# Attention and a gated MLP in one kernel: the softmax maxima reach the query rows by sixteen direct transfers, from an earlier place, in a new order of a period's products

## The chip, the cores and the metric

The kernel runs on one core of one Trainium2 chip. The metric is device time in microseconds for one execution; before the change it is 1812.37 us (median of 3 runs, 1811.87 to 1816.35). Five engines matter: PE (TensorE, matrix products, with its weight loads PEld), DVE (VectorE), ACT (ScalarE), POOL (GpSimd) and SP (SyncE), which here only issues DMA transfers from one queue.

## The reference

```python
x = A_x                                             # [1, 2048, 512], float32
g = sigmoid((x * gate_w).sum(-1, keepdims=True))
# a: full attention, 32 heads of 16
qkv = (x @ wqkv).reshape(B, S, 3, 32, 16).transpose(2, 0, 3, 1, 4)
p = softmax(einsum("bhqd,bhkd->bhqk", q, k) * 16 ** -0.5)
a = einsum("bhqk,bhkd->bhqd", p, v).transpose(0, 2, 1, 3).reshape(B, S, 512) @ wo
# b: gated MLP, 512 -> 1792 -> 512
b = (sigmoid(x @ w_gate) * (x @ w_up)) @ w_down
return g * a + (1 - g) * b
```

Both branches read the same `x`. Every score row needs its own maximum before the exponential.

## The kernel before, in words

**Pairs, halves, periods.** Two heads form a pair `p` (16 pairs): one uses the lower 64 rows of the PE array (`b = 0`), the other the upper 64 (`b = 1`). A pair's 2048 queries are two halves `i` of 1024. The main loop runs over 256 periods `k`; eight periods handle one half of one pair. The queries of a pair lie in a tile `QS` with heads along partitions, the keys in `KS`.

**Maxima by an extra row.** The scores are computed twice. Ten periods ahead (`FIRST = 20` steps), `sm_step` forms them with queries along partitions (L250) and DVE takes row maxima (L252) into `stat`; after 64 of them a last reduction (L256) yields `m`, the maxima of one half: 128 partitions, 2 heads, 8 blocks of 128 queries. Later `st_part` forms the scores again, transposed, with keys along partitions (L460), and ACT exponentiates them out of PSUM (L462). So that nothing has to be subtracted there, each head's query rows in `QS` carry two more rows (partitions `64 b + 48` and `64 b + 49`) with the maximum, split in a high and a low part, and the key rows carry -1 against them. These two rows per head must be in `QS` before the first transposed product of a half.

**The way of the maxima.** `split_max` (L260) splits `m` into `mhl` on POOL (a cast, L94, and a subtraction, L95). `turn_max` (L265) transposes `mhl` in 32 x 32 blocks on DVE (L269), stores the result to a DRAM buffer `m_d` (L270, 16 KB) and loads it back into the four rows of `QS` (L275, four loads of 4 KB each, in pieces of 128 bytes), `b = 0` first. All transfers are issued by SP, in one order.

**A period.** `emit` (L517) walks through the words of `STEADY`, one product each: `t0` and `t1` are transposed scores of the two heads (`t1` one period ahead of `t0`), `m0` and `m1` score products for maxima, `d0` and `d1` halves of a dense product (`Sum`) in the bank `dn` that belongs to the projections and to the MLP. The suffix is the half of the PE array; products of different halves run at once. A dense product has 12 terms and takes two periods. `turn` stands for a POOL no-op that hands `dn` from one half to the other, for one piece of queued POOL work, and for `turn_max` if a split is waiting. After the words come the next dense run, two more pieces of POOL work (`work(2)`), and `values(k)` (L467): eight products of probabilities with `v`, on all 128 rows. At the very end `split_max` is recorded.

**Banks.** Apart from `dn`, seven PSUM banks serve the 17 products of a period that need one. `place` (L511) hands them out: `REUSE` says for each of the 17 places how many hand-outs back its bank was last given. A product waits until the bank's former reader (ACT for `t` and values, DVE for `m`) is done.

**Order.** PE, ACT, DVE and POOL run in the order in which the code is written; SP's order is set by the scheduler. In the first 48 periods the dense products are projections of q and k: their results are split by POOL (L120, L117) and stored by SP (L207). Later ones are MLP columns, stored at L305. `load_pair` (L210) loads the next pair's rows.

In the prediction, the turn period is the one after a half's maxima are complete, in which the transpose is done; the stall period is the next, in whose middle the first `t1` needs the new rows.

Of the kernel before, what the change touches and what calls it, by code (L numbers as in the profile page):

```python
# [11 lines left out]
F32 = mybir.dt.float32  # L12
F32R = mybir.dt.float32r
# [11 lines left out]
P = 128  # L25
# [4 lines left out]
NPAIR = H // 2  # L30
# [13 lines left out]
def gated_mix(ctx, tc, x, xc, wqk, wv, wo, w_gu, w_down, gate_w, out):  # L44
    nc = tc.nc
    pe, act, dve, pool, sp = nc.tensor, nc.scalar, nc.vector, nc.gpsimd, nc.sync

    ctx.enter_context(tc.manual_schedule(engines=ORDERED))
    keep = ctx.enter_context(tc.tile_pool(name="keep", bufs=1))
    dram = ctx.enter_context(tc.tile_pool(name="dram", bufs=1, space=DRAM))  # L50
# [18 lines left out]
    gu_d = dram.tile([2, NF, P, S], F32, name="gu_d")  # L69
    pv_d = dram.tile([2, NPAIR, P, 512], F32, name="pv_d")  # L70
    rec_d = dram.tile([P, 512], F32, name="rec_d")
    m_d = dram.tile([NPAIR, 2, P, 32], F32, name="m_d")

    warm = keep.tile([P, 1], F32, name="warm")
    dve.memset(warm, 0.0)
# [14 lines left out]
    def split(h, l, src, hi, lo):  # L90
        if hi is act:
            act.activation(h, src, AF.Copy)  # L92
        else:
            hi.tensor_copy(h, src)  # L94
        lo.tensor_tensor(l, src, h.bitcast(F32), ALU.subtract)  # L95
# [72 lines left out]
    QS, KS = zip(*[(big(f"qs{b}", F32R), big(f"ks{b}", F32R)) for b in range(2)])  # L168
# [64 lines left out]
    mrow = {}  # L233
# [24 lines left out]
        return one  # L258

    def split_max(half):  # L260
        hl = keep.tile([P, 2, 16], F32R, name=f"mhl{half[0]}_{half[1]}", tag="mhl", bufs=2)
        split(hl[:, 0, :], hl[:, 1, :], mrow.pop(half).rearrange("p a b -> p (a b)"), pool, pool)
        turning.append((half, hl))

    def turn_max():  # L265
        half, hl = turning.pop(0)
        p, i = half
        mt = keep.tile([P, 32], F32, name=f"mt{p}_{i}", tag="mt", bufs=2)
        dve.transpose(mt, hl.rearrange("p a b -> p (a b)").bitcast(F32))  # L269
        sp.dma_start(m_d[p, i], mt)  # L270
        rows = m_d[p, i].rearrange("(g a b t) j -> a b t g j", g=4, a=2, b=2)
        for b in range(2):
            for a in range(2):
                r = 64 * b + 3 * DH + a
                sp.dma_start(QS[p % 2][r:r + 1, i * 1024:(i + 1) * 1024].bitcast(F32).rearrange(  # L275
                    "o (t g j) -> o t g j", g=4, j=32), rows[a, b].unsqueeze(0))

    turning = []

# [45 lines left out]
    for c in range(NC):  # L325
# [9 lines left out]
        for w, dst in ((w_q, q_d), (w_k, k_d)):  # L335
            o = bank()
# [20 lines left out]
    for t in range(2):  # L357
        o = bankv()
# [90 lines left out]
    def st_part(k, b):  # L449

        p, r = divmod(2 * k, 32)
        i, kt = divmod(r, 16)
        qs, ks = QS[p % 2], KS[p % 2]
        r = 64 * b
        pt = ptile[k, b] = mid(f"p{k}_{b}")
        for a in range(2):
            for c in range(2):
                o = bank()
                q0 = i * 1024 + c * 512
                pe.matmul(o, ks[r:r + KR, (kt + a) * P:(kt + a + 1) * P], qs[r:r + KR, q0:q0 + 512],  # L460
                          start=True, stop=True)
                act.activation(pt[:, 2 * a + c, :], o, AF.Exp, scale=DH ** -0.5)  # L462
                yield
# [47 lines left out]
    def place():  # L511
        b = given[-REUSE[count_given[0] % len(REUSE)]]
        count_given[0] += 1
        given.append(b)
        return b

    def emit(order, **parts):  # L517

        for word in order.split():
            if word == "turn":  # L520
                turn(run)
                work(1)
                if turning:
                    turn_max()
            else:
                next(parts[word], None)

    STEADY = ("t0 m1 d1 m0 t0 d1 d1 m0 d1 t0 d1 m0 d1 turn t0 t1 m0 "
              "d0 m1 m1 d0 d0 t1 d0 t1 t1 d0 d0 m1")
    REUSE = (5, 8, 6, 6, 10, 7, 7, 6, 8, 7, 7, 6, 8, 6, 8, 7, 7)  # L530
    LAST = ["t0 d1 t0 d1 t0 d1 d1 turn t0 t1 t1 d0 t1 d0 t1 d0 d0"] * (TAIL - 4) + [
        "t0 d1 t0 d1 t0 d1 turn t0 t1 t1 d0 t1 d0 t1 d0"] * 4

# [10 lines left out]
    for k in range(NPER):  # L544
        n = 2 * k
        if n + FIRST == NSTEP:
            bank = bank7
            leave = dve.tensor_copy
        if 128 <= n < 256 and n % 16 == 0:
            logit_load((n - 128) // 8)  # L550
        if 128 <= n < 256 and n % 16 in (6, 8):
            logits((n - 128) // 16 * 2, (n % 16 - 6) // 2)
        if n % 32 == 0 and n // 32 + 1 < NPAIR:
            load_pair(n // 32 + 1)
        parts["t0"], parts["t1"] = st_part(k, 0), st_part(k + 1, 1) if k + 1 < NPER else iter(())
        emit(STEADY if k < NPER - TAIL else LAST[k - NPER], **parts)
        if k == NPER - 1:
            bankd = bank
        if run.done():
            run = next(fill)  # L560
        else:
            turn(run)
        work(2)
        if k == NPER - 1:
            break
        values(k)
        for half in list(mrow):
            split_max(half)
        if n == NSTEP - 16:
            loaded.extend(hidden_load(*chunks[m]) for m in range(2))  # L570
            raws = [late_raw(*late[m][:2]) for m in range(2)]
        if n == NSTEP - 10:
            denominators(0)
# [86 lines left out]
    for n, (c, f) in enumerate(chunks):  # L660
# [4 lines left out]
        hl = ready[n]  # L665
# [49 lines left out]
```

## Time and profile before

| | |
|---|---|
| median of 3 runs | 1812.37 us (1811.87 to 1816.35) |
| the profiled execution | 1814.77 us, span 1813.0 us |
| mean granted TensorE clock | 0.991 |
| PE busy | 1753.0 us, 97% of the span |
| DVE, ACT, POOL busy | 1417.8, 1341.6, 467.6 us |
| from 260 to 1000 us of the span | PE 713.91, DVE 631.28, ACT 610.63 of 740 us |
| waits of PE for the maxima rows | 34.3 us (20 times) and 18.0 us (11 times) |

The span runs from the first to the last instruction; the execution's own time lies 1.8 us above it. Rows of a timeline give start, duration, engine, line, operation and, in brackets, how long the engine stood idle before and what ended it; `x4` merges four instructions. Rows of stretches give the stretch, its length, busy time and count of PE, PEld, DVE, ACT and POOL, then the granted TensorE clock, the share of the DMA engines and GB/s. A DMA row on SPq is the time of issue, not of the transfer.

### The profile page before, as it was taken

The numbers are of one execution on the slowest core, as the hardware profiler recorded it, in microseconds if no ns is written. First come the engines' busy times: TensorE is split into PE (matmuls) and PEld (weight loads), VectorE is DVE, ScalarE is ACT, GpSimd is POOL, SyncE is SP. The second block draws the span as 40 slices with busy tenths as digits, with TensorE's granted clock in tenths as the row PEclk, the third lists the DMA queues.
The fourth block names the chain that finished last, engine by engine and source line by source line (L and its number), as shares of the span: only waits on it lengthen the run. The fifth ranks groups of instructions, "written<-read, shape, count | busy, mean of one in ns | idle before, by whom it ended". The sixth has DMA issues, their size and how long they took to land.

```text
span 1813.0 us, 33225 instructions
## 1 busy us (share of the span) xinstructions
PE 1753.0 (97%) x12676; PEld 1046.7 (58%) x12676; DVE 1417.8 (78%) x2282; ACT 1341.6 (74%) x2564; POOL 467.6 (26%) x435
## 2 busy tenths in 40 slices
PE   9999999999999999999999999999999999999999
PEld 7755555555555555555555555555555555488887
DVE  5987787788888888888888888888888887156543
ACT  4187787788888888788888888888888888953321
POOL 1034343332222222222222222222222222352110
PEclk9999999999999999999999999999999999999999
DMA  9212324141313131313131212112121212277752
GB/s 253 68 37 65 77 65 89 48 112 37 72 48 83 48 83 48 78 48 82 38 65 43 59 49 56 46 51 55 45 54 45 63 43 77 72 237 245 249 187 74
DMA packets 84959, 149.22 MB, mean 82 GB/s; under 512 B 18816, under 2 KB 27008, under 8 KB 81792
## 3 DMA queue, kind: packets, MB, share of 16 engines
q1 hardware_dynamic: 84512, 146.58, 29.6%
q8 instruction: 99, 1.62, 0.4%
q14 instruction: 60, 0.49, 0.1%
q10 hardware_dynamic: 288, 0.52, 0.1%
HBM read 87.56 MB, written 59.51 MB: 81 GB/s over the span
## 4 chain that ended last, share of the span: by engine, by line
PE 84%; DMA 6%; DVE 5%; SPq 3%; issue 1%; ACT 0%; POOL 0%; POOLq 0%
PE dn L143 14%; PE sm L475 13%; PE sm L460 11%; PE st L475 10%; PE sm L250 8%; PE st L460 8%; PE sm L670 7%; DVE stat L252 5%; PE st L250 4%; PE st L130 4%; SPq L275 3%; DMA qs<-m_d 3%; DMA m_d<-mt 3%; PE dn L670 2%; PE st L143 1%; PE sm L579 1%
## 5 line engine op out<-in xcount | busy, mean ns | idle before, releaser
L252 DVE TENSOR_REDUCE stat<-sm 128x1 f32<-128x512 f32 x1188 | 766.3, 681 | 110.0 <-PE sm L250 85.5
L462 ACT ACTIVATE p<-sm 128x512 f32<-128x512 f32 x1190 | 675.4, 622 | 35.9 <-PE st L250 26.5
L252 DVE TENSOR_REDUCE stat<-st 128x1 f32<-128x512 f32 x860 | 567.4, 680 | 119.7 <-PE st L250 101.4
L490 POOL TENSOR_TENSOR sum<-sum,part 128x512 f32<-128x512 f32 x224 | 287.9, 1285 | 920.5 <-PE sm L460 624.7
L462 ACT ACTIVATE p<-st 128x512 f32<-128x512 f32 x858 | 498.4, 623 | 24.6 <-PE st L250 13.8
L460 PE MATMUL sm<-qs,ks 64*128 64x512 f32 x1190 | 476.2, 424 | 35.1 <-DMA qs<-m_d 34.3
L250 PE MATMUL sm<-ks,qs 48*128 48x512 f32 x1188 | 475.1, 435 | 0.2
L250 PE MATMUL st<-ks,qs 48*128 48x512 f32 x860 | 364.4, 445 | 0.0
L460 PE MATMUL st<-qs,ks 64*128 64x512 f32 x858 | 342.7, 419 | 19.9 <-DMA qs<-m_d 18.0
L460 PEld LDWEIGHTS sm<-qs,ks 64*128 64x128 f32 x1190 | 221.0, 186 | 215.8 <-ACT p L462 97.0
L475 PE MATMUL sm<-p,v 128*17 128x512 f32 x2096 | 250.7, 595 | 0.0
L250 PEld LDWEIGHTS sm<-ks,qs 48*128 48x128 f32 x1188 | 214.1, 186 | 51.3 <-DVE stat L252 31.8
L475 PE MATMUL st<-p,v 128*17 128x512 f32 x2000 | 242.4, 602 | 0.0
L460 PEld LDWEIGHTS st<-qs,ks 64*128 64x128 f32 x858 | 159.0, 186 | 120.6 <-ACT p L462 49.8
L250 PEld LDWEIGHTS st<-ks,qs 48*128 48x128 f32 x860 | 155.2, 186 | 29.7 <-DVE stat L252 20.5
L479 ACT ACTIVATE part<-st 128x512 f32<-128x512 f32 x124 | 75.2, 607 | 103.8 <-issue 88.6
L475 PEld LDWEIGHTS sm<-p,v 128*17 128x17 f32 x2096 | 48.8, 97 | 122.9 <-issue 81.5
L475 PEld LDWEIGHTS st<-p,v 128*17 128x17 f32 x2000 | 46.6, 97 | 122.0 <-issue 84.4
L479 ACT ACTIVATE part<-sm 128x512 f32<-128x512 f32 x100 | 61.7, 617 | 67.4 <-issue 63.1
L424 DVE TENSOR_TENSOR gul<-gul 128x1024 f32<-128x1024 f32 (+1 forms) x30 | 46.0, 1538 | 35.0 <-ACT gul L423 32.4
L670 PE MATMUL sm<-wd_h,hl 128*128 128x512 f32 x208 | 68.3, 395 | 0.0
L92 ACT ACTIVATE hl<-gul 128x1024 fp32r<-128x1024 f32 (+1 forms) x30 | 29.9, 996 | 43.4 <-PE sm L670 29.7
(455 smaller groups left out, 2998.7 us busy)
## 6 DMA issues: line engine op xcount, KB each, us to landing
gu_d<-gu SPq DMA_DIRECT2D x112, 256.0 KB
gul<-gu_d SPq DMA_DIRECT2D x56, 512.0 KB
qs<-q_d SPq DMA_DIRECT2D x90, 128.0 KB
ks<-k_d SPq DMA_DIRECT2D x90, 128.0 KB
pv_d<-sum SPq DMA_DIRECT2D x32, 256.0 KB
q_d<-qe SPq DMA_DIRECT2D x12, 512.0 KB
k_d<-qe SPq DMA_DIRECT2D x12, 512.0 KB
x<-in_xc_dram SPq DMA_DIRECT2D x16, 256.0 KB
```

Of the source, the lines that this page charges most:

```text
L130: pe.matmul(o, a, b, start=(i == 0), stop=(i == len(ops) - 1))
L143: mm = pe.matmul(self.o, a[rows], b[rows], start=(self.n == 0), stop=(self.n == 2 * len(self.ops) - 1))
L250: pe.matmul(t, qs[r:r + KM, qt * P:(qt + 1) * P], ks[r:r + KM, g * 512:(g + 1) * 512], start=True, stop=True)
L252: dve.tensor_reduce(stat[half][:, b, qt % 8, g:g + 1], t, axis=AX.X, op=ALU.max)
L275: sp.dma_start(QS[p % 2][r:r + 1, i * 1024:(i + 1) * 1024].bitcast(F32).rearrange("o (t g j) -> o t g j", g=4, j=32), rows[a, b].unsqueeze(0))
L424: dve.tensor_tensor(gu[:, 1, a], gu[:, 0, a], gu[:, 1, a], ALU.mult)
L460: pe.matmul(o, ks[r:r + KR, (kt + a) * P:(kt + a + 1) * P], qs[r:r + KR, q0:q0 + 512], start=True, stop=True)
L462: act.activation(pt[:, 2 * a + c, :], o, AF.Exp, scale=DH ** -0.5)
L475: pe.matmul(o[32 * c:32 * c + VW, :], v[:, 2 * k % 16 + a, h * VW:(h + 1) * VW], pts[c // 2][:, 2 * a + c % 2, :], start=(a == 0), stop=(a ...
L479: act.activation(e, o, AF.Copy)
L490: pool.tensor_tensor(s, s, e, ALU.add)
L670: pe.matmul(down[t], a, b, start=(f == 0 and m == 0), stop=(f == NF - 2 and m == 5))
```

## The change

Four things change. `split_max` is recorded before a period's end work instead of after `values(k)`. `turn_max` is recorded at the start of the next period, before its first product, instead of at `turn` in its middle. The buffer `m_d` goes: `mhl` is laid out so that 8 partitions of the transposed tile hold the pieces of one row for one residue `g`, and sixteen transfers go straight from the transposed tile to the rows of `QS`, each 8 pieces of 128 bytes. And `STEADY` and `REUSE` get new values.

```diff
-    m_d = dram.tile([NPAIR, 2, P, 32], F32, name="m_d")
...
     def split_max(half):
-        hl = keep.tile([P, 2, 16], F32R, name=f"mhl{half[0]}_{half[1]}", tag="mhl", bufs=2)
-        split(hl[:, 0, :], hl[:, 1, :], mrow.pop(half).rearrange("p a b -> p (a b)"), pool, pool)
+        hl = keep.tile([P, 2, 2, 8], F32R, name=f"mhl{half[0]}_{half[1]}", tag="mhl", bufs=2)
+        split(hl[:, :, 0, :], hl[:, :, 1, :], mrow.pop(half), pool, pool)
         turning.append((half, hl))
 
     def turn_max():
         half, hl = turning.pop(0)
         p, i = half
         mt = keep.tile([P, 32], F32, name=f"mt{p}_{i}", tag="mt", bufs=2)
-        dve.transpose(mt, hl.rearrange("p a b -> p (a b)").bitcast(F32))
-        sp.dma_start(m_d[p, i], mt)
-        rows = m_d[p, i].rearrange("(g a b t) j -> a b t g j", g=4, a=2, b=2)
+        dve.transpose(mt, hl.rearrange("p b a t -> p (b a t)").bitcast(F32))
         for b in range(2):
             for a in range(2):
                 r = 64 * b + 3 * DH + a
-                sp.dma_start(QS[p % 2][r:r + 1, i * 1024:(i + 1) * 1024].bitcast(F32).rearrange(
-                    "o (t g j) -> o t g j", g=4, j=32), rows[a, b].unsqueeze(0))
+                row = QS[p % 2][r:r + 1, i * 1024:(i + 1) * 1024].bitcast(F32).rearrange(
+                    "o (t g j) -> o t g j", g=4, j=32)
+                for g in range(4):
+                    c = 32 * g + 16 * b + 8 * a
+                    sp.dma_start(row[:, :, g, :], mt[c:c + 8, :])
...
             if word == "turn":
                 turn(run)
                 work(1)
-                if turning:
-                    turn_max()
             else:
                 next(parts[word], None)
 
-    STEADY = ("t0 m1 d1 m0 t0 d1 d1 m0 d1 t0 d1 m0 d1 turn t0 t1 m0 "
-              "d0 m1 m1 d0 d0 t1 d0 t1 t1 d0 d0 m1")
-    REUSE = (5, 8, 6, 6, 10, 7, 7, 6, 8, 7, 7, 6, 8, 6, 8, 7, 7)
+    STEADY = ("t0 m1 d1 m0 t0 d1 m0 d1 d1 t0 d1 m0 d1 turn t0 t1 m0 "
+              "m1 d0 d0 t1 m1 d0 d0 t1 d0 t1 d0 m1")
+    REUSE = (6, 5, 9, 6, 9, 7, 7, 6, 8, 6, 8, 6, 8, 6, 8, 7, 7)
...
         parts["t0"], parts["t1"] = st_part(k, 0), st_part(k + 1, 1) if k + 1 < NPER else iter(())
+        if turning:
+            turn_max()
         emit(STEADY if k < NPER - TAIL else LAST[k - NPER], **parts)
+        for half in list(mrow):
+            split_max(half)
         if k == NPER - 1:
             bankd = bank
         if run.done():
...
         values(k)
-        for half in list(mrow):
-            split_max(half)
```

What moves on the engines, at the places of which the prediction speaks. DVE at the turn of pair 7's second half, before the change (`stat` are the maxima of one half, `m` their last reduction, `mhl` the split, `mt` the transposed tile; the names `sm` and `st` on the right are PSUM banks):

```order
L256 TENSOR_REDUCE m_1_8472<-stat_1_7980 128x16
L252 TENSOR_REDUCE stat_0_8493<-st_67 128x1
L252 TENSOR_REDUCE stat_0_8493<-st_65 128x1
L252 TENSOR_REDUCE stat_0_8493<-st_66 128x1
L252 TENSOR_REDUCE stat_0_8493<-sm_69 128x1
L269 STREAM_TRANSPOSE mt_1_8514<-mhl_1_8487 128x32
L252 TENSOR_REDUCE stat_0_8493<-st_65 128x1
```

and with the change:

```order
L255 TENSOR_REDUCE m_1_8636<-stat_1_8151 128x16
L268 STREAM_TRANSPOSE mt_1_8654<-mhl_1_8638 128x32
L251 TENSOR_REDUCE stat_0_8675<-sm_72 128x1
L251 TENSOR_REDUCE stat_0_8675<-sm_69 128x1
L251 TENSOR_REDUCE stat_0_8675<-sm_71 128x1
```

The transpose moves from behind the fourth maximum of the next half to straight behind the reduction.

SP at the same place, before (`gu_d` is the store of an MLP column):

```order
L305 DMA gu_d<-gu_1_0_8474 128x512
L270 DMA m_d<-mt_1_8514 128x32
L275 DMA qs_108<-m_d 1x32x32 x4
L99 DMA g6r<-in_w_gu_dram 128x512
L305 DMA gu_d<-gu_1_1_8605 128x512
```

and with the change:

```order
L305 DMA gu_d<-gu_1_0_8641 128x512
L276 DMA qs_107<-mt_1_8654 1x8x32 x16
L98 DMA g6r<-in_w_gu_dram 128x512
L305 DMA gu_d<-gu_1_1_8780 128x512
```

One store and four loads become sixteen transfers at the same place of the queue.

SP in the first phase, second half of pair 1, with the change (`q_d` is the store of a projected and split q; before, it stood ahead of the store to `m_d`):

```order
L206 DMA k_d<-qe_0_2253 128x2x512
L276 DMA qs_107<-mt_1_2395 1x8x32
L206 DMA q_d<-qe_1_2381 128x2x512
L276 DMA qs_107<-mt_1_2395 1x8x32 x15
L206 DMA k_d<-qe_1_2523 128x2x512
```

Fifteen of the sixteen transfers stand behind the store of q, which waits for POOL. This is so in six halves: the second of pair 0, both of pairs 1 and 2, and the first of pair 3.

## The prediction

> **What bounds the kernel now.** I read the waits first, then stretches of single periods, then the timeline round one turn of maxima, then the issue times of the transfers. Busy time by engine from the page, and four rows of the waits (total us, times, longest):
>
> ```profile
> PE 1753.0 (97%) x12676; PEld 1046.7 (58%) x12676; DVE 1417.8 (78%) x2282; ACT 1341.6 (74%) x2564; POOL 467.6 (26%) x435
> ...
> PE sm L460 <- DMA qs<-m_d: 34.3, 20, 3.4
> PE st L460 <- DMA qs<-m_d: 18.0, 11, 2.8
> ...
> PEld sm L250 <- DVE stat L252: 31.8, 136, 0.4
> PEld st L250 <- DVE stat L252: 20.5, 92, 0.2
> ```
>
> TensorE sets the end. It loses 52.3 us in 31 waits for the maxima that come back into the query rows, one per half pair, and about 0.23 us in nearly every period (228 waits) for a PSUM bank that VectorE still reads. Four consecutive periods, stretch and length first, PEclk third from last; then the sum lines of the same view over the six stall periods of the first phase (two of them shown whole) and over the 24 after it:
>
> ```profile
> 879.62:885.23 5.61, 5.61 (x48) 3.15 (x44) 5.01 (x9) 5.05 (x10) 1.29 (x1) 1.00 0.01 3
> 885.23:890.87 5.64, 5.64 (x48) 3.14 (x44) 5.05 (x10) 4.58 (x9) 1.71 (x3) 1.00 0.14 49
> 890.87:897.75 6.88, 5.66 (x50) 3.16 (x46) 4.96 (x8) 5.22 (x10) 3.10 (x3) 1.00 0.09 11
> ...
> 131.75:143.45 11.70, 8.29 (x48) 4.11 (x45) 5.06 (x8) 5.22 (x10) 3.14 (x3) 0.71 0.01 1
> 182.75:192.38 9.63, 7.08 (x48) 4.08 (x44) 5.06 (x8) 5.22 (x10) 2.13 (x3) 0.82 0.27 44
> ...
> sum 58.03, PE 42.18 PEld 22.18 DVE 30.16 ACT 31.31 POOL 13.86; mean PE 7.03 PEld 3.70 DVE 5.03 ACT 5.22 POOL 2.31
> ...
> sum 171.98, PE 136.75 PEld 75.45 DVE 119.36 ACT 125.25 POOL 52.36; mean PE 5.70 PEld 3.14 DVE 4.97 ACT 5.22 POOL 2.18
> ```
>
> An ordinary period takes 5.61, the turn period (second row) 5.64, the stall period after it 6.88. Turn and stall period together cost 5.64 + 171.98/24 = 12.81 in 24 halves and 5.64 + 58.03/6 = 15.31 in the six early ones. The timeline of that turn, from T = 885.23 (the row of a DMA is from the chain of waits):
>
> ```profile
> 885.10 0.22 DVE L256 TENSOR_REDUCE m<-stat 128x16 f32<-128x64 f32 x1
> 885.23 0.50 PE L460 MATMUL st<-qs,ks 64*128 64x512 f32 x1
> 885.38 0.20 POOL L94 CAST mhl<-m 128x16 fp32r<-128x16 f32 x1 [2.33 <-DVE m L256]
> 885.66 0.22 POOL L95 TENSOR_TENSOR mhl<-m,mhl 128x16 fp32r<-128x16 f32 x1
> 885.80 1.29 DVE L252 TENSOR_REDUCE stat<-st 128x1 f32<-128x512 f32 x2 [0.48 <-PE st L250]
> 888.20 0.20 DVE L269 STREAM_TRANSPOSE mt<-mhl 128x32 f32<-128x32 f32 x1
> 888.33 0.65 DVE L252 TENSOR_REDUCE stat<-st 128x1 f32<-128x512 f32 x1
> 888.43 0.32 SPq L270 DMA_DIRECT2D m_d<-mt  x1
> 889.85 2.78 SPq L275 DMA_DIRECT2D qs<-m_d  x4
> 891.98 1.90 DMA qs<-m_d
> 892.39 0.40 PE L460 MATMUL sm<-qs,ks 64*128 64x512 f32 x1
> 894.01 0.47 PE L460 MATMUL sm<-qs,ks 64*128 64x512 f32 x1 [1.22 <-DMA qs<-m_d]
> ```
>
> The split is done at T+0.65, but the transpose stands in the middle of the period (T+2.97). The store lands, four loads are issued one each 0.695 (2.78 and a gap, over 4), the last lands at 893.88, 1.25 after its issue ends (891.98 + 0.65), and TensorE goes on 0.13 later, at T+8.78. Without a stall the matmul would come 0.23 after the one at 892.39: the stall is 1.39, and 3.74 remain to the period's end (897.75).
>
> **The change, part by part.** *Earlier turn.* VectorE now transposes straight after the last maxima, so it waits for POOL's T+0.65: from about T+0.70 to T+0.90. The next maxima queue behind it; their first read moves from T+0.57 to about T+0.83 (the transpose costs 0.13 net, 888.20 to 888.33). The products that end a period wait for the fifth read, so the turn period grows to about 5.80. The first matmul that needs the new rows stands 1.73 into a period (892.62 less 890.87), so without a stall it is due at T+5.80+1.73 = T+7.53. POOL's earlier place costs nothing in this phase: it stood idle 2.33 before the split.
>
> *Sixteen direct transfers.* The store (0.32 and 1.1 of landing) and four loads go; the first new issue can start at T+0.93. All is decided by what one issue costs, since the first stalled matmul needs the upper rows, which are the last eight of sixteen on SP's one queue. No row shows a transfer from SBUF to SBUF. Issue times of groups (min/median/max ns), and six issues in a row:
>
> ```profile
> L216 SPq DMA_DIRECT2D qs<-q_d x102: 302/418/797, 23.8 to 1410.1; - x102
> L275 SPq DMA_DIRECT2D qs<-m_d x128: 649/650/814, 79.7 to 1541.2; - x128
> L442 SPq DMA_DIRECT2D xn<-in_x_dram x8: 383/384/500, 397.6 to 733.0; - x8
> L621 SPq DMA_DIRECT2D ot<-pv_d x32: 577/577/641, 1608.6 to 1768.7; - x32
> ...
> 944.85 2.73 SPq L216 DMA_DIRECT2D ks<-k_d  x6
> ```
>
> Below: 302, the shortest issue of all, one each 0.347 with the gap of 45 ns that lies between issues. Above: 649, today's write of the same kind of row in the same 128-byte pieces. In a run, 16-row loads go out one each 0.463 (2.73 over 6, gap included), 418 apiece. L275 and L621 are the groups whose outermost size is 8 on one side; L621 costs about 200 more than L442, which has 128 there and as many dimensions. The new transfers are 8 pieces on both sides: shaped simply like L216, but with the 8. 302 + 200 gives 502, the run's price 418; I take 0.46, so one each 0.505.
>
> [...]
>
> *Sum of a turn.* The rows arrive at 0.93 + 15 x 0.505 + 0.46 + 1.20 + 0.13 = T+10.30 (1.20 for the landing: 1.25 above, 1.10 for the store, whose issue ends at 888.75 and which frees the loads at 889.85). Turn and stall period: 10.30 + 3.74 = 14.04 instead of 12.81: +1.23. The stall is 10.30 - 7.53 = 2.77, about 2.6 of idleness.
>
> *Clock.* In the early stall periods idleness is length less PE busy. At 2.55 and 3.41 (rows above) PEclk fell to 0.82 and 0.71, and PE's busy time rose from 5.6 to 7.08 and 8.29: +1.5 and +2.7. The third of the six shows the other side:
>
> ```profile
> 231.71:239.57 7.86, 5.56 (x49) 3.01 (x45) 4.96 (x8) 5.22 (x10) 1.53 (x2) 1.00 0.02 4
> 378.27:386.37 8.10, 5.58 (x50) 3.05 (x46) 4.96 (x8) 5.22 (x10) 1.54 (x2) 1.00 0.30 53
> ```
>
> 2.30 and 2.52 idle cost nothing. At 2.6 I count +1.5. [...]
>
> *Order of a period.* An ordinary period, from 914.51, on PE, VectorE, ScalarE and the weight loads:
>
> ```profile
> 914.51 0.50 PE L460 MATMUL sm<-qs,ks 64*128 64x512 f32 x1
> 916.43 0.50 PE L250 MATMUL st<-ks,qs 48*128 48x512 f32 x1
> ...
> 915.69 2.47 DVE L252 TENSOR_REDUCE stat<-st 128x1 f32<-128x512 f32 x4
> ...
> 915.19 2.56 ACT L462 ACTIVATE p<-sm 128x512 f32<-128x512 f32 x5
> ...
> 918.28 0.13 PEld L475 LDWEIGHTS st<-p,v 128*17 128x17 f32 x8 [0.30 <-DVE stat L252]
> ```
>
> The first maxima matmul after the period's middle (916.43) waits for VectorE's second read to end (915.69 + 0.68 = 916.37). In the new bank numbers it follows a bank that ScalarE's second exponential leaves at 915.19 + 0.49 + 0.60 = 916.28: 0.09 sooner. The closing products still take the bank of the fifth read, which ends at 918.16; with the same 0.06 they could start at 918.21 instead of 918.28. The gain is between 0 and 0.09 a period; I take 0.06, so 0.36 in the six ordinary periods of a half. If other banks come late instead, nothing hides it: 0.06 worse would cost 245 x 0.06 = 15 us.
>
> *The six early halves.* There the split of a projected q, two long POOL instructions, stood before the maxima; now it stands behind them, and its store stands on SP after the first of the sixteen:
>
> ```profile
> 176.81 0.61 POOL L120 CAST qe<-qk 128x512 fp32r<-128x512 f32 x1 [1.88 <-ACT qk L312]
> 177.50 1.30 POOL L117 TENSOR_TENSOR qe<-qk,qe 128x512 fp32r<-128x512 f32 x1
> 178.75 0.19 POOL L94 CAST mhl<-m 128x16 fp32r<-128x16 f32 x1
> ...
> 178.83 0.36 SPq L207 DMA_DIRECT2D q_d<-qe  x1
> ```
>
> Cast and subtraction now end near T+2.69 (0.70 + 0.61 + 0.08 + 1.30), the store is issued to T+3.08, and the other fifteen follow it: arrival 3.13 + 14 x 0.505 + 0.46 + 1.33 = T+12.0. The pair: 15.74 for 15.31, +0.43, and +2.7 of clock, as after 3.41 idle.
>
> *Sum.* 25 halves (the 24 and the one that ends the loop): 1.23 + 1.5 - 0.36 = 2.37 each, 59 us. Six: 0.43 + 2.7 - 0.36 = 2.77 each, 17 us. Together +76. It is made against the profiled execution (span 1813.0, 1814.8 in all, 2.4 above the median), so I add it to the median: 1812.4 + 76 = 1888.
>
> **The rivals.** *Cheap issues (faster).* If the price follows the simple shape alone, 0.302 and 0.347: arrival T+7.77, pair 11.51, -1.30 - 0.36 = -1.66, times 25 = -41; early arrival T+9.62, -1.95 - 0.36 = -2.31, times 6 = -14. That is 1757. For it: every group with 16 or more on both sides can be issued in 302 to 384. Against it: 16-row loads in a run take 418, and no group with an 8 is below 577. It decides below about 0.42 from issue to issue.
>
> *Full price.* If the pieces and the 8 make the price, 0.649 and 0.694: arrival T+13.3, pair 17.06, +4.25 + 2.7 - 0.36 = 6.6, times 25; early T+14.8, 5.6 times 6: +199, 2011. For it: L275 is the nearest row in every respect but the dimensions of its source. Against it: L621 is 72 ns cheaper with as many dimensions, so shape counts.
>
> *No change.* Between 0.42 and 0.44 the longer queue eats what the hop gave. The doubt on the period's order (15 us either way) lies inside these cases.
>
> **How the numbers follow.** Issues at 0.44 to 0.60: 0.50, own range 1820 to 1965 (at 0.60: 490 per us of spacing from 25 x 16 + 6 x 15, 47 more than above, and 30 more of clock). Cheap: 0.33. Full price: 0.12. No change: 0.05. A measurement can tell 0.3%, 5.4 us, from no change: faster 0.33, same 0.05, slower 0.62. The range takes in the cheap end and leaves most of the full price out: 1752 to 1965.
>
> **What would show it.** The new transfers' issue time and spacing: below 0.42 proves me wrong. The wait of the first matmul on the new rows: about 2.6 us forecast, under 0.3 in the cheap case, over 5 at full price. PEclk in stall periods: about 0.8 forecast, 1.00 if cheap. The turn period near 5.80, the ordinary one near 5.55; above 5.61 the order is a loss.

## The result and the profile after

The changed kernel takes 2004.66 us (median of 4 runs, 2003.44 to 2007.61) against 1814.30 us for the kernel before (median of 4 runs, 1811.87 to 1816.35): a ratio of 1.1052, 95% interval 1.1031 to 1.1074. It is slower, as forecast, but by 190 us instead of 76, and it lies outside the predicted range.

The profiled execution takes 2004.56 us, with a span of 2002.8 us and a mean granted TensorE clock of 0.943. From the page: the busy times (share of the span, instructions), and the shares of the chain that ended last (the work that set the end, followed back from the last instruction), first with the change and then before it.

```profile
PE 1816.4 (91%) x12676; PEld 1122.7 (56%) x12676; DVE 1422.6 (71%) x2282; ACT 1332.0 (67%) x2564; POOL 466.0 (23%) x435
...
PE 70%; SPq 15%; DVE 9%; DMA 3%; issue 2%; POOL 1%; ACT 0%; POOLq 0%
...
PE 84%; DMA 6%; DVE 5%; SPq 3%; issue 1%; ACT 0%; POOL 0%; POOLq 0%
```

The work is the same, 12676 matrix instructions. PE's share fell from 97% to 91%, and its busy time still rose by 63 us, since part of the work now runs at a lower clock (0.943 in the mean, 0.991 before). In the chain SPq has grown from 3% to 15%: issuing transfers has become a larger part of what sets the end. The waits (total us, times, longest):

```profile
PE st L460 <- DMA qs<-mt: 180.1, 32, 7.5
...
PEld st L475 <- DVE stat L251: 87.9, 246, 0.7
...
DVE mt L268 <- POOL mhl L94: 19.1, 32, 0.6
...
PEld sm L249 <- DVE stat L251: 11.4, 43, 0.4
```

The 52.3 us of waits for the maxima rows have become 180.1 us in 32 waits, 5.6 us each. The closing products' short wait for VectorE, once a period, is still there; the wait of the maxima products for it, 52.3 us in 228 waits before, has shrunk to 11.4 in 43. VectorE now waits 0.6 us for POOL's split at each turn, as the sum of the turn period assumed.

The same turn as in the prediction, that of pair 7's second half, starts here at T = 876.21. First the issue times of the sixteen transfers over the whole kernel (min/median/max ns); then SP's row for this turn and, from the chain of waits, the last transfer; then, from PE's timeline, the matmul that waited for it.

```profile
L276 SPq DMA_DIRECT2D qs<-mt x512: 634/635/1301, 77.0 to 1729.3; - x171
...
877.14 11.17 SPq L276 DMA_DIRECT2D qs<-mt  x16
...
887.68 1.68 DMA qs<-mt
...
889.50 0.77 PE L460 MATMUL st<-qs,ks 64*128 64x512 f32 x1 [5.56 <-DMA qs<-mt]
```

The first issue starts at T+0.93, exactly where the prediction put it. But an issue takes 0.635 us, one each 0.68 with the gap, where I had taken 0.46 and 0.505. The sixteenth starts at 887.68, ends at 888.31 and has landed at 889.36, 1.05 later; PE goes on at 889.50, T+13.29, after 5.56 us of idleness. At this turn the second issue took 0.95 us; over the 24 late halves PE goes on at T+13.1 on average.

Stretches: an ordinary period, the turn period, the stall period and the one behind it; then an early stall period and two late ones for comparison; then the sum over all 31 stall periods (columns as in the table before the prediction).

```profile
864.75:870.36 5.61, 5.61 (x48) 3.40 (x44) 5.50 (x11) 4.51 (x9) 1.30 (x1) 1.00 0.41 140
876.21:882.04 5.83, 5.83 (x48) 3.12 (x45) 5.07 (x10) 4.51 (x9) 1.71 (x3) 1.00 0.16 52
882.04:896.06 14.02, 8.46 (x49) 4.12 (x46) 5.11 (x8) 5.32 (x10) 3.08 (x3) 0.76 0.13 38
896.06:901.67 5.61, 5.61 (x49) 3.39 (x46) 4.88 (x8) 4.51 (x9) 1.29 (x1) 1.00 0.13 47
...
133.71:148.73 15.02, 8.28 (x49) 4.11 (x46) 5.11 (x8) 5.33 (x10) 3.14 (x3) 0.66 0.01 3
1199.39:1211.64 12.25, 7.03 (x48) 4.00 (x44) 5.11 (x8) 5.32 (x10) 3.08 (x3) 0.86 0.11 27
1251.12:1264.75 13.63, 8.41 (x50) 4.11 (x46) 5.11 (x8) 5.33 (x10) 1.26 (x1) 0.75 0.25 57
...
sum 419.27, PE 240.97 PEld 124.49 DVE 153.40 ACT 164.72 POOL 72.11; mean PE 7.77 PEld 4.02 DVE 4.95 ACT 5.31 POOL 2.33
```

The six early stall periods sum to 90.70, the one that ends the loop takes 13.63, so the other 24 take 13.12 on average, where before they took 7.17. The early ones take 15.12. With turn periods of 5.82, a late turn and stall period cost 18.94 instead of 12.81 and an early pair 20.94 instead of 15.31: 25 x 6.13 + 6 x 5.63 = 187 of the 190 us. Nearly all of the loss lies there. The ordinary period is 5.61 as before: the new order of products has gained nothing.

### The profile page after: what moved, and what is told of

It reads as the page before. It is cut to its first block, busy times and chain, and to the rows that moved or that the text cites. A ratio compares the mean times of both kernels' runs of the same rounds, so it can differ in the third digit from the quotient of the medians.

```text
span 2002.8 us, 33699 instructions
## 1 busy us (share of the span) xinstructions
PE 1816.4 (91%) x12676; PEld 1122.7 (56%) x12676; DVE 1422.6 (71%) x2282; ACT 1332.0 (67%) x2564; POOL 466.0 (23%) x435
## 4 chain that ended last, share of the span: by engine, by line
PE 70%; SPq 15%; DVE 9%; DMA 3%; issue 2%; POOL 1%; ACT 0%; POOLq 0%
PE st L475 18%; SPq L276 14%; PE dn L142 13%; PE st L460 9%; DVE stat L251 8%; PE sm L670 6%; PE sm L460 6%; PE sm L249 6%; PE st L129 4%; DMA qs<-mt 3%; PE st L249 3%; PE dn L670 1%; PE st L142 1%; PE sm L579 1%; PE sm L475 1%
## 5 line engine op out<-in xcount | busy, mean ns | idle before, releaser
L251 DVE TENSOR_REDUCE stat<-sm 128x1 f32<-128x512 f32 x1433 | 901.6, 682 | 209.0 <-PE sm L249 186.0
L462 ACT ACTIVATE p<-st 128x512 f32<-128x512 f32 x1021 | 616.4, 642 | 186.6 <-PE st L249 169.7
L460 PE MATMUL st<-qs,ks 64*128 64x512 f32 x1021 | 460.2, 454 | 181.6 <-DMA qs<-mt 180.1
L462 ACT ACTIVATE p<-sm 128x512 f32<-128x512 f32 x1027 | 600.5, 648 | 17.7 <-PE dn L142 17.7
L249 PE MATMUL sm<-ks,qs 48*128 48x512 f32 x1433 | 570.8, 434 | 0.2
L251 DVE TENSOR_REDUCE stat<-st 128x1 f32<-128x512 f32 x615 | 401.7, 682 | 181.4 <-PE st L249 161.6
L475 PE MATMUL st<-p,v 128*17 128x512 f32 x3984 | 500.1, 622 | 0.0
L249 PE MATMUL st<-ks,qs 48*128 48x512 f32 x615 | 281.2, 457 | 0.0
L479 ACT ACTIVATE part<-st 128x512 f32<-128x512 f32 x217 | 130.8, 603 | 224.1 <-issue 197.4
L249 PEld LDWEIGHTS sm<-ks,qs 48*128 48x128 f32 x1433 | 252.5, 191 | 33.8 <-DVE stat L251 11.4
L312 ACT ACTIVATE gu<-dn 128x512 f32<-128x512 f32 x99 | 66.9, 676 | 0.0
```

The costliest lines, as they stand in the source:

```text
L249: pe.matmul(t, qs[r:r + KM, qt * P:(qt + 1) * P], ks[r:r + KM, g * 512:(g + 1) * 512], start=True, stop=True)
L251: dve.tensor_reduce(stat[half][:, b, qt % 8, g:g + 1], t, axis=AX.X, op=ALU.max)
L312: leave = lambda e, o: act.activation(e, o, AF.Copy)
L475: pe.matmul(o[32 * c:32 * c + VW, :], v[:, 2 * k % 16 + a, h * VW:(h + 1) * VW], pts[c // 2][:, 2 * a + c % 2, :], start=(a == 0), stop=(a ...
L479: act.activation(e, o, AF.Copy)
```

## The experiments

**The early turn alone.** The kernel before, with the split recorded ahead of the end work and the transpose at the start of the next period; the store, the four loads and the old order of products stay.

```diff
-                if turning:
-                    turn_max()
...
+        if turning:
+            turn_max()
         emit(STEADY if k < NPER - TAIL else LAST[k - NPER], **parts)
+        for half in list(mrow):
+            split_max(half)
...
         values(k)
-        for half in list(mrow):
-            split_max(half)
```

> The kernel before with the split and the turn at their new, earlier places; the store to the buffer in DRAM, the four loads and the old order of a period stay. Theory A (what was lost is the sixteen issues of 0.635 us, one each 0.68, on one queue ahead of the first product that needs the rows; the earlier turn alone is a gain): the rows arrive at T+0.93 + 0.32 + 1.10 + 4 x 0.695 + 1.38 = T+6.5, before they are due at T+7.5, so no stall; turn period 5.82, stall period 5.61, together 11.43 instead of 12.81 in 25 halves and instead of 15.31 in the six early ones: -35 and -23, about 1756 us. Rival B (VectorE waiting for POOL ahead of its maxima, or the earlier turn otherwise, costs more than it gives): turn periods well over 6 us, no gain, 1812 us or more.

Measured: 1762.28 us (1760.84 to 1762.64) beside 1812.98, ratio 0.9718 (0.9698 to 0.9739). Stretches from an ordinary period to the one behind the turn, and SP's rows for that turn (T = 895.77):

```profile
890.15:895.77 5.62, 5.62 (x48) 3.13 (x44) 5.01 (x9) 5.07 (x10) 1.29 (x1) 1.00 0.00 1
895.77:901.60 5.83, 5.82 (x50) 3.05 (x46) 5.05 (x10) 4.62 (x9) 1.71 (x3) 1.00 0.16 53
901.60:907.21 5.61, 5.61 (x48) 3.13 (x44) 4.88 (x8) 5.07 (x10) 1.29 (x1) 1.00 0.41 71
...
896.69 0.32 SPq L270 DMA_DIRECT2D m_d<-mt  x1
898.11 2.78 SPq L275 DMA_DIRECT2D qs<-m_d  x4
```

The store starts at T+0.92, the last load's issue ends at T+5.12, and with 1.25 of landing and 0.13 the rows are there at about T+6.5, a microsecond before the first matmul needs them. The stall period has become an ordinary one. This part of the change gains 50.7 us by itself, and this kernel is faster than the kernel before and the changed one. The expectation was 58 (35 and 23); four stall periods that still take 6.1 to 6.4 us account for 3 of the 7 us that are missing, and the rest was not traced.

**The early turn with the new order.** The same, with the new `STEADY` and `REUSE`.

> As e1, with the new order of a period and the new bank numbers: the whole change without the sixteen transfers. Theory A with a neutral order (the ordinary periods of the changed kernel take 5.61 as before): the same as e1 within 3 us, about 1756. Rival C (the order gains 0.06 a period, hidden in the changed kernel by something the transfers do): 15 us under e1. Rival D (the order costs): over e1.

Measured: 1761.84 us (1760.21 to 1762.36), ratio 0.9716 (0.9699 to 0.9733). The two kernels differ by 0.4 us, less than their runs do among themselves. The order of products bears nothing of the result.

**The upper rows first.** The changed kernel, with the rows of the upper half of the array sent before the lower ones.

```diff
-        for b in range(2):
+        for b in (1, 0):
```

> The changed kernel with the sixteen transfers in the other order of heads: the eight of the upper head, which is needed first, ahead of the eight of the lower. Theory A (issue time in a queue): the upper rows arrive near T+7.5, just in time; the lower ones near T+13.1 and are due a period later, at T+11.4: a stall of about 1.7 a half, no fall of the clock. Turn, stall and next period together 0.4 above the kernel before in 25 halves, 0.8 below in six: about 1819 us. Rival E (small transfers between two places of SBUF land slowly or hinder each other, so that the last landing counts and not the place in the queue): still near 2004, at least above 1950.

Measured: 1827.39 us (1823.98 to 1829.36), ratio 1.0077 (1.0056 to 1.0098). Its waits for the rows:

```profile
PE sm L460 <- DMA qs<-mt: 45.8, 27, 2.7
...
PE st L460 <- DMA qs<-mt: 12.2, 12, 2.0
```

58.0 us of waits instead of 180.1, with the same 512 transfers at the same price (0.635 us). The time is 8 us above the expected one and far from the 1950 of rival E. The 177 us between this kernel and the changed one come from the place in the queue alone: what counts is when the first half that is needed has landed.

**Eight transfers of sixteen pieces.** The changed kernel, with the two rows of a head in one transfer.

```diff
-            for a in range(2):
-                r = 64 * b + 3 * DH + a
-                row = QS[p % 2][r:r + 1, i * 1024:(i + 1) * 1024].bitcast(F32).rearrange(
+            r = 64 * b + 3 * DH
+            row = QS[p % 2][r:r + 2, i * 1024:(i + 1) * 1024].bitcast(F32).rearrange(
                     "o (t g j) -> o t g j", g=4, j=32)
-                for g in range(4):
-                    c = 32 * g + 16 * b + 8 * a
-                    sp.dma_start(row[:, :, g, :], mt[c:c + 8, :])
+            for g in range(4):
+                c = 32 * g + 16 * b
+                sp.dma_start(row[:, :, g, :], mt[c:c + 16, :])
```

> The changed kernel with the high and the low part of a head in one transfer: eight transfers of 16 pieces, two rows at the destination, so that the outermost sizes are 2 and 16. [...]

Measured: 1764.34 us (1763.93 to 1766.58), ratio 0.9734 (0.9716 to 0.9751). The issue times and the wait:

```profile
L275 SPq DMA_DIRECT2D qs<-mt x256: 598/611/842, 76.4 to 1489.0; - x128
...
PE st L459 <- DMA qs<-mt: 8.3, 7, 1.9
```

An issue of twice the bytes and twice the pieces costs 0.611 us, slightly less than the 0.635 before: here the price is paid per transfer. At 0.70 an issue, a little over the 0.635, the author's estimate was about 1780 us. At 0.611 it comes out lower: 0.93 + 7 x 0.655 + 0.61 + 1.33 = T+7.46 is just ahead of the T+7.53 at which the rows are due, so the late halves, but for the last, do not stall at all: their stall periods take 5.6 us, the six early ones 6.6. The time alone would have spoken for cheap issues, for which the prediction has 1757 us; only the issue row decides. Halving the count of the same kind of transfer takes 240 us away, which shows that the sixteen issues are the loss.

**The sixteen transfers alone.** The kernel before with the changed `split_max` and `turn_max` (the first piece of the diff of the change), but everything recorded at its old place and in the old order.

> The kernel before with the sixteen direct transfers alone: the split stays behind the values, the transpose in the middle of the period, the old order of products stays. If the changed kernel's loss is the sixteen issues and the earlier place only takes off from it, the rows arrive at T + 3.2 + 15 x 0.68 + 0.635 + 1.33 = T + 15.4 instead of about T + 13.1, so each of 31 halves is 2.2 us longer than in the changed kernel (less 0.2 for the shorter turn period), and the clock stays low longer, 0 to 1.7 us a half: 2065 to 2120. If the early place itself costs something that I do not see (VectorE's or SyncE's order), it ends below 2005.

Measured: 2054.29 us in one run, beside 1812.30. Its waits for the rows:

```profile
PE sm L460 <- DMA qs<-mt: 156.2, 20, 8.2
...
PE st L460 <- DMA qs<-mt: 86.3, 12, 8.2
```

It ends 11 us below the expected range, but 49.6 us above the changed kernel, where the rival wanted it below. The transfers cost 242.0 us at the old place (2054.29 - 1812.30), and 242.4 at the new one (2004.66 - 1762.28); the early turn gains 50.7 with the loads and 49.6 with the transfers. The two parts add up, and no further cause is needed. The miss comes from the six early halves, where the early place gains little because the other fifteen transfers stand behind the store of q: stall periods of 15.0 to 15.3 there in the changed kernel and 15.2 to 15.8 here.

**What an issue costs.** Three kernels carry bursts of six small transfers on SP's queue, whose data nobody reads, on top of the early turn; each line of a diff here is one burst, for `u` from 0 to 5, and only those are shown whose rows follow. Those shown move pieces of 128 bytes. The first has SBUF at both ends.

```diff
+                sp.dma_start(one_row(u, 8), probes[32:40, :])
+                sp.dma_start(probed[48:64, cols], probes[64:80, :])
+                sp.dma_start(probed[64:76, cols], probes[32:44, :])
+                sp.dma_start(probed[80:82, cols], probes[32:34, :])
```

> This is the kernel with the early turn alone and nine added bursts, of six small transfers each, from a tile of zeros in SBUF to a scratch tile in SBUF that nobody reads; every transfer is made of 128-byte pieces. Shapes: 8, 16, 32 or 4 pieces from as many partitions into one row; 8, 16, 12, 2 or 1 partitions to as many partitions. Theory S (what makes an issue dear is an outermost size that does not divide by 16): the rows of 16 and of 32 pieces and the 16 to 16 partitions issue in 0.30 to 0.42 us, all others in 0.58 to 0.66, and 12, 4, 2 and 1 cost about what 8 does. Rival R (the write into one partition is dear): all four shapes into one row take about 0.635, all five from partitions to partitions 0.30 to 0.42. Rival D (the way from SBUF to SBUF is dear): all nine take about 0.635. The time itself: about 1762, since nothing waits for the bursts.

Measured, in order 8 pieces into one row, then 16, 12 and 2 partitions to as many partitions:

```profile
L537 SPq DMA_DIRECT2D probed<-probes x6: 623/632/659, 85.9 to 89.4; - x6
...
L547 SPq DMA_DIRECT2D probed<-probes x6: 536/587/589, 117.0 to 120.1; - x6
...
L549 SPq DMA_DIRECT2D probed<-probes x6: 713/714/786, 120.7 to 124.6; - x6
...
L551 SPq DMA_DIRECT2D probed<-probes x6: 562/563/601, 125.3 to 128.4; - x6
```

My theory of the outermost size is wrong: 16 pieces cost 0.587, nearly as much as 8. The other five shapes lie between 0.573 and 0.634 too. What all nine share is SBUF at both ends. The second kernel sets that against the rival that small transfers are dear.

```diff
+                sp.dma_start(probed[0:16, cols], probe_d[6, 64:80, :])
+                sp.dma_start(probed[32:40, cols], probe_d[6, 64:72, :])
+                sp.dma_start(probed[:, 256 + 32 * u:288 + 32 * u], probes[:, :32])
+                sp.dma_start(probed[:, 512 + 32 * u:544 + 32 * u], probe_d[6])
+                sp.dma_start(probe_e[u, 64:80, :], probe_d[6, 64:80, :])
```

> Again the kernel with the early turn alone and nine bursts of six small transfers. The first set of bursts showed 0.56 to 0.71 us for every transfer from SBUF to SBUF, even with 16 on both sides. Now: 16 and 8 pieces of 128 bytes from DRAM to SBUF; 16 and 8 from SBUF to DRAM; 128 pieces from SBUF to SBUF, from DRAM to SBUF, from SBUF to DRAM; 16 from DRAM to DRAM; and 16 pieces of 256 bytes from SBUF to SBUF. Theory D (SBUF at both ends makes an issue dear): 16 pieces to or from DRAM, 128 pieces to or from DRAM and DRAM to DRAM issue in 0.30 to 0.45, and 128 pieces from SBUF to SBUF cost 0.59 or more. Rival M (few or small pieces make it dear): all bursts of 8 and 16 pieces cost 0.55 to 0.65 whatever the ends, and all three of 128 pieces 0.30 to 0.45. In both, 8 pieces cost at least as much as 16. The time itself: about 1762.

Measured, in order: 16 pieces from DRAM to SBUF, 8 likewise, 128 from SBUF to SBUF, 128 from DRAM to SBUF, 16 from DRAM to DRAM.

```profile
L537 SPq DMA_DIRECT2D probed<-probe_d x6: 303/418/420, 89.9 to 92.1; - x6
...
L539 SPq DMA_DIRECT2D probed<-probe_d x6: 283/298/325, 92.6 to 94.3; - x6
...
L545 SPq DMA_DIRECT2D probed<-probes x6: 557/599/599, 97.5 to 100.7; - x6
...
L547 SPq DMA_DIRECT2D probed<-probe_d x6: 427/430/592, 101.3 to 103.8; - x6
...
L551 SPq DMA_DIRECT2D probe_e<-probe_d x6: 474/590/808, 107.2 to 111.0; - x6
```

Between partitions of SBUF and DRAM, in both directions, an issue costs 0.29 to 0.30 for 8 pieces and 0.42 to 0.43 for 16 and for 128; from SBUF to SBUF it costs 0.59 and 0.60 for the same 16 and 128, and 0.59 for 16 pieces of 256 bytes. So SBUF at both ends is dear at every size tried here, and rival M falls. Nor is it a queue that fills up: the one transfer of the changed kernel that goes out alone in an early half takes 0.64 as well (its row stands further below). In one point theory D is too narrow: DRAM at both ends is as dear. And 8 pieces from DRAM are cheaper than 16, against what both theories expected. Why the two ends matter is not shown.

That leaves the four loads of the kernel before, which cost 0.65 with DRAM at one end.

```diff
+            far = probe_d[u].rearrange("(g a t) j -> a t g j", g=2, a=8)[0]
+            near = probe_d[u]
...
+                sp.dma_start(probed[u:u + 1, :].rearrange("o (t g j) -> o t g j", g=2, j=32), far.unsqueeze(0))
+                sp.dma_start(probed[8 + u:9 + u, :].rearrange("o (t j) -> o t j", j=32), near[:16].unsqueeze(0))
+                sp.dma_start(probed[32:40, 64 * u:64 * u + 64].rearrange("o (g j) -> o g j", j=32), far)
+                sp.dma_start(probed[48:64, 64 * u:64 * u + 64].rearrange("o (g j) -> o g j", j=32),
+                             near[:32].rearrange("(g t) j -> t g j", g=2))
```

> Once more the kernel with the early turn alone and added bursts of six small loads from DRAM to SBUF, in pieces of 128 bytes. It asks why the four loads of the kernel before cost 0.65 us each, when 8 or 16 plain pieces from DRAM cost 0.29 and 0.42. Shapes: into one row 16 pieces in two levels (8 by 2); into one row 16 pieces in one level, 8 pieces in one level; into 8 partitions two pieces each; into 16 partitions two pieces each; into one row 16 pieces in two levels (2 by 8). Theory L (a second level of pieces makes an issue dear): both rows in two levels and the 8 and 16 partitions with two pieces each take 0.55 to 0.70, the two plain rows 0.29 to 0.43. Rival R (the write into one row is dear): the four shapes into one row take 0.55 to 0.70, the two into partitions 0.29 to 0.45. If neither, no shape takes over 0.45, and the price of those loads comes from their place or their count of pieces. The time itself: about 1762.

Measured, in order: 16 pieces into one row in two levels (8 by 2), 16 pieces into one row in one level, and 8 partitions and 16 partitions with two pieces each.

```profile
L538 SPq DMA_DIRECT2D probed<-probe_d x6: 649/650/672, 89.1 to 92.7; - x6
...
L540 SPq DMA_DIRECT2D probed<-probe_d x6: 247/248/421, 93.4 to 95.0; - x6
...
L544 SPq DMA_DIRECT2D probed<-probe_d x6: 276/297/308, 97.0 to 98.7; - x6
...
L546 SPq DMA_DIRECT2D probed<-probe_d x6: 422/426/813, 104.7 to 107.5; - x6
```

Neither theory holds. The second level is not dear in itself (0.297 and 0.426), nor is the write into one row (0.248), but both together are: 0.650, and 0.589 for 2 by 8. The plain rows are in one piece in DRAM as well, so a row gathered in one level from scattered pieces was not tried. Why this case shares the price of the transfers within SBUF stays open; that the 0.65 came from the shape of those loads and not from their place is shown. The three kernels take 1762.01, 1761.04 and 1754.72 us in one run each. That the first comes out as expected is partly luck: in its first stall period, 14.9 us long, the rows of the maxima wait behind the bursts, and it makes up for half of that behind the main loop, where it and the third are 5 us shorter than the others, for a reason that stays open.

**What sets the ordinary period.** The early turn alone, with VectorE reading only the first 256 of each 512 score columns: half of the keys is left out of the maxima, while all products are computed.

```diff
-            dve.tensor_reduce(stat[half][:, b, qt % 8, g:g + 1], t, axis=AX.X, op=ALU.max)
+            dve.tensor_reduce(stat[half][:, b, qt % 8, g:g + 1], t[:, :256], axis=AX.X, op=ALU.max)
```

> The kernel with the early turn alone, in which VectorE reads only the first 256 of each 512 score columns for the maxima, so half of the keys is left out of the maxima (the products are all computed). It asks what sets the ordinary period at 5.61. Theory V (VectorE's reads, one each 0.60, whose fifth lets the closing products start): a read falls to about 0.35 to 0.40, the closing products no longer wait for it, and the period falls to what TensorE's own products or ScalarE's 5.05 allow, 5.2 to 5.4: 1762 - 245 x 0.2 to 0.4 = 1664 to 1713. Rival P (TensorE's own products fill 5.61): the period stays, 1757 to 1763.

Measured: 1734.49 us (1733.34 to 1734.95), ratio 0.9570 (0.9540 to 0.9600). Two consecutive stretches:

```profile
927.83:933.38 5.55, 5.55 (x48) 3.11 (x44) 3.10 (x8) 5.00 (x10) 3.13 (x3) 1.00 0.00 0
933.38:938.94 5.56, 5.56 (x49) 3.12 (x45) 3.10 (x8) 4.52 (x9) 1.29 (x1) 1.00 0.50 144
```

VectorE's work in a period falls from about 4.9 to 3.10, and the period only from 5.61 to 5.55. Both theories miss: VectorE's reads account for 0.06 of a period (and for the 0.2 of the turn period, which is gone), and the rest is set elsewhere. By what is not shown: TensorE is busy for all of the 5.55, ScalarE for 5.00, and TensorE's weight loads now wait nearly once a period for the POOL no-op that hands over `dn` (71.5 us in 243 waits, 0.7 in 2 with full reads). So in this order of products the length of VectorE's reads costs 0.06 an ordinary period.

> The same with the new order of a period's products and the new bank numbers. Theory V says that the order did not matter because VectorE's fifth read set the period in both; with that out of the way the order may show: I expect it within 0.1 us a period of the old order, 25 us either way, and not the same to 1 us. Rival P: the order makes no difference here either, within 2 us of the run with short reads and the old order.

Measured: 1735.93 us (1735.28 to 1737.54), ratio 0.9580 (0.9555 to 0.9606), with the same periods of 5.55. With short reads, too, the new order gains nothing. But VectorE is not out of the way in this order, as it was in the old one, where the closing products waited 1.8 us for it in all:

```profile
PEld st L475 <- DVE stat L252: 60.0, 246, 0.4
```

So the run tells nothing of what the order would do without VectorE.

**The transpose behind the first maximum.** The early turn alone, but the transpose stands behind VectorE's first read of the period, so that it finds the split done. Beside it, the early turn once more.

```diff
             else:
                 next(parts[word], None)
+                if word == "m1" and turning:
+                    turn_max()
...
-        if turning:
+        if turning and k >= NPER - TAIL:
             turn_max()
```

> The kernel with the early turn alone, but the transpose stands behind the period's first maximum instead of ahead of it, so that VectorE no longer waits for POOL's split (0.60 us idle in the run of the early turn). If that wait is what lengthens the turn period to 5.82, it falls to 5.65 to 5.75 (0.13 for the transpose stays); the rows arrive about 0.6 later, near T + 7.1, still before T + 7.4: 31 x 0.07 to 0.17 = 2 to 5 us less than the run beside it, 1757 to 1760. Rival: the transpose itself lengthens the period, wherever it stands ahead of the fifth read: no change, within 1 us; or the later rows come too late in some halves and the gain is eaten: 1762 to 1770.

> The kernel with the early turn alone once more, on the same chip as the run beside it, to compare the two: 1762, within 2 us, by every theory.

Measured: 1792.19 us (1787.58 to 1792.98), ratio 0.9869 (0.9850 to 0.9889), and 1760.78 us (1760.50 to 1762.16) for the early turn, ratio 0.9705 (0.9688 to 0.9721). The turn period does fall, from 5.82 to 5.71, about 3 us over the kernel. But the six early stall periods grow to between 9.9 and 10.9 us. SP's rows at one of them, here first with the later transpose and then with the early one:

```profile
179.17 0.36 SPq L207 DMA_DIRECT2D q_d<-qe  x1
179.62 0.42 SPq L270 DMA_DIRECT2D m_d<-mt  x1
182.96 2.77 SPq L275 DMA_DIRECT2D qs<-m_d  x4
```

```profile
172.25 0.33 SPq L270 DMA_DIRECT2D m_d<-mt  x1
173.92 0.37 SPq L207 DMA_DIRECT2D q_d<-qe  x1
174.38 2.78 SPq L275 DMA_DIRECT2D qs<-m_d  x4
```

With the later transpose the store of the maxima stands behind the store of q on SP's queue, not ahead of it, and its loads start 2.9 us after the end of its issue (182.96 less 180.04). In most later halves of the kernel before, with no store of q ahead, it is 1.1. The six periods lose 27 us, eight times the gain of the turn period: here, too, the place in the queue decides.

## Why the prediction was wrong in size, point by point

**The step that failed: the price of an issue.** "I take 0.46, so one each 0.505" should have been 0.635 and 0.68. Put into the prediction's own sum, 0.93 + 15 x 0.68 + 0.635 + 1.33 gives T+13.10, as the late halves show on average. (At the turn shown, T+13.29, the long second issue added 0.31, and the way from the last issue to the matmul took 0.14 less than counted.) That is 2.8 us more than the forecast T+10.30 in each late half, 70 us in 25, and 2.6 in each of the six early ones (14.6 for 12.0), 16 us. The argument went from the shape: a simple pattern like the loads of L216, with a surcharge for the outermost size of 8. The bursts show what was wrong with it. The 8 costs 0.045 over the 16 where both ends are SBUF, and from DRAM it is cheaper than the 16; the price is that of SBUF at both ends, which no row of the kernel before shows. The nearest row in size was L275, for another reason. One reading behind the 0.46 was wrong as well: that every group with 16 or more on both sides can be issued in 0.302 to 0.384. In the trace of the kernel before, L434, a load of 64 rows into 64 partitions, takes 0.474 and 0.524.

**The rival that came true** is "Full price", at 0.649 and 0.694: it gave 2011, and 2004.66 was measured. Its price came true, but not its reason, that the pieces and the 8 make the price: between two places of SBUF 16 and 128 pieces cost nearly as much. That it comes within 6 us is partly luck, since its gain from the order of products (11 us too much) and its loss of clock (some 15 too much) nearly cancel. It had a chance of 0.12, with the reason against it that L621 is cheaper than L275, "so shape counts". L621 is another load from DRAM, and could say nothing of a transfer without one. Where the trace bounds an unknown price by rows that all differ from it in the same respect, the upper end deserved as much as the middle.

**The clock** was right in kind: it falls in long stalls (PEclk 0.66 to 0.86 in the 31 stall periods, 1.00 in the turn period shown), and in the late halves that cost more than was counted. By the forecast arrival the stall would have been 2.77 and cost 1.5 of lower clock; with an arrival at T+13.10 the stall period would be 13.10 + 3.74 - 5.82 = 11.02 at full clock, and is 13.12: 2.1 a late half. In the early halves, forecast at 2.7, an arrival near T+14.6 (3.13 + 14 x 0.68 + 0.635 + 1.33) would give 12.5 at full clock; 15.1 stands there, 2.6 more. But the rule by which 1.5 was chosen does not hold: that a stall of 2.55 costs it and one of 2.52 nothing. The fourth of the early stall periods of the kernel before, which the prediction does not show, was idle for 2.51 us (11.08 less 8.57), had the lowest clock of all six, and lost 3.0 us of PE's time (8.57 less the 5.58 at full clock):

```profile
278.87:289.95 11.08, 8.57 (x48) 4.12 (x45) 5.06 (x8) 5.22 (x10) 3.14 (x3) 0.69 0.23 37
```

The length of a stall alone does not tell what it costs; the last section comes back to this.

**The order of a period**, taken at a gain of 0.06, gains nothing: 11 us of the forecast. The wait of the maxima products at which it aimed did shrink, from 52.3 to 11.4 us, but that of the closing products grew from 75.3 to 87.9. The rows of the ordinary period at 864.75:

```profile
865.57 1.89 DVE L251 TENSOR_REDUCE stat<-sm 128x1 f32<-128x512 f32 x3
867.37 1.28 DVE L251 TENSOR_REDUCE stat<-st 128x1 f32<-128x512 f32 x2
...
868.76 0.13 PEld L475 LDWEIGHTS st<-p,v 128*17 128x17 f32 x8 [0.30 <-DVE stat L251]
```

The closing products still wait for VectorE's fifth read, which ends at 868.65, and follow it 0.11 later. The prediction noted that this bank is the same in both orders, and still carried the gain of an earlier product through to the end of the period.

**What held.** The turn period was to be 5.80 and is 5.82. The transfers start at T+0.93, as computed. From the end of the last issue to the waiting matmul it takes 1.05 + 0.14 where 1.33 was counted. The store of q stands ahead of fifteen of the sixteen in the early halves, and is issued at T+2.6 where 2.7 was derived, as SP's rows for the second half of pair 1 show (T = 182.38):

```profile
183.31 0.64 SPq L276 DMA_DIRECT2D qs<-mt  x1
184.99 0.36 SPq L206 DMA_DIRECT2D q_d<-qe  x1
185.40 10.17 SPq L276 DMA_DIRECT2D qs<-mt  x15
```

And that the upper rows decide, being the last eight in the queue, is shown by the kernel that sends them first.

**The sum.** Of the 187 us worked out from the pairs, the prediction had 76. Of the 111 that were missing, the issues are 86, the order 11 and the lower clock 14 (25 halves at 2.1 instead of 1.5).

## What to carry to other kernels

Cost a new kind of transfer by its two ends before its bytes: here one from SBUF to SBUF took 0.56 to 0.71 us of its queue whether it moved 256 bytes or 16 KB, and a plain one between SBUF and DRAM 0.29 to 0.43, so sixteen direct transfers took longer than one store and four loads. Many issues on one queue set their own end (sixteen took 11.17 us of it here); what is needed first has to stand first, and half as many transfers of the same kind, twice as large, took 240 us away. And a change of several parts should be timed part by part: the early turn here was worth 51 us, and was hidden by 242 us of transfers.

## What the runs showed of the hardware that was not expected

**Issue times on SP's queue** in runs of six: 0.25 for one piece of up to 2 KB from DRAM into a row; 0.29 to 0.30 for 8 and 0.42 to 0.43 for 16 or 128 pieces between DRAM and partitions; 0.56 (2 pieces), 0.57 (4), 0.63 (8), 0.71 (12), 0.59 (16) and 0.60 (128) from SBUF to SBUF; 0.59 from DRAM to DRAM (16); 0.59 to 0.65 for a row gathered from DRAM in two levels.

**The clock fell in fixed steps.** While it was low it was half: from 138 to 148, from 889 to 895.5 and from 1207 to 1209 us of the changed kernel the granted clock is 0.50. So the share of the clock that was lost in a stall period, times its length, over one half, is the time at half clock: 0.14 x 12.25 / 0.5 = 3.4 us, 0.24 x 14.02 / 0.5 = 6.7 us and 0.34 x 15.02 / 0.5 = 10.2 us. All 31 stall periods lie within 0.3 us of one of the three. What a stall cost was not set by its length alone: two stalls of the same 5.22 us (12.25 less 7.03, and 13.63 less 8.41) differ by 1.4 us of PE's time.

**A small store behind a large one** landed late. From the end of the issue of the 16 KB store of the maxima to the first load that depends on it takes 2.9 us in the early half shown of the kernel with the later transpose, where the 512 KB store of q was issued 0.1 us ahead of it; 2.1 to 3.3 in the six early halves of the kernel before, where it was issued 1.1 us ahead; and 1.1 in most of its halves without it. Some of those take up to 2.7 too, so a large store just ahead is not the only cause.
